# Earlier PV and projections, and residuals on VectorE, in a two-layer attention and token-mixing kernel

## The chip, the cores and the metric

The kernel runs on one core of one Trainium2 chip. The metric is the device time of that core in microseconds, from the program's start to its end. The profile's span runs from the first to the last instruction of one execution.

## The reference

The input has 2048 tokens of 1024 features in bf16. The network applies an attention block A and a token-mixing block B, and then both again with the same weights.

```
x = x + A(layernorm(x));  x = x + B(layernorm(x))      # layer 0
x = x + A(layernorm(x));  x = x + B(layernorm(x))      # layer 1

A: q, k, v = h @ wqkv      (32 heads of 32)
   a token looks at 8 tokens: itself and 2, 4, ... 14 before it
   o = softmax(q . k / sqrt(32)) v ;  result o @ wo    (1024 x 1024)
B: u = gelu(h^T @ w1 + b1)     mixes 2048 tokens into 3584
   y = u @ w2 + b2             and back into 2048 tokens
```

Since the window steps by two, even and odd tokens never meet in the attention. The kernel treats them as two classes of 1024 tokens. Block B mixes all of them.

## The kernel before

**Attention.** The class `Attn` works in four head groups per layer, numbered n = 0 to 3. Groups 0 and 1 belong to class 0, groups 2 and 3 to class 1. A group has four blocks (`dq`) of 128 features, that is four heads each. For a group the steps are:

- `qk_proj`: q and k are projected by TensorE (L400), two blocks at a time (8 units of 8 matmuls), and copied out of PSUM by ScalarE (L404, L407). There are only two q and two k buffers, so the projection of the next two blocks waits until `qk` has read these.
- `qk`: VectorE multiplies q with the shifted k (T, L430, 2.2 us, two per block), and TensorE sums over the features with a 0/1 matrix (sc, L435).
- `softmax_front` and `softmax_back`: maxima, exponentials and the quotient on VectorE and ScalarE, ending in Pb (L455). GpSimd's queue stores Pb to DRAM (pd, L458) and loads it back, spread over the partitions, in two halves (pb, L472).
- `v_proj`: v is projected (L400, four units per pair of blocks).
- `pv`: per block and half, two products of 128x2048 (L490) and then three adds that halve the width (L501, L501, L503), all on VectorE. For the pairs named in `pe_pv` the adds are eight identity matmuls (L496) and a copy by ScalarE (L498). Before the change this holds for blocks 2 and 3 of group 1 in layer 0.

`stream` writes these steps in a fixed order: during group n it does `pv` of group n-1. One exception is called `turn`: q and k of group 2, the first of class 1, are projected only after everything else of group 1. They need the normalized and transposed rows of class 1 (hT), which the fill `second` makes, so the step begins with a "drain" of `second`.

**Fills.** `weave` mixes this lead with fills, in this order once they are opened: `second` (layer 0: norm of class 1; layer 1: the last matmul of layer 0, `gemm2_tile`, for class 1), `v_ahead` (v of class 1, 16 units), `out0` (`out_proj` of class 0, eight tiles), `partials` and `late` (24 and 16 units of `gemm1` over class 0 alone). `out0` and `partials` open when `pv` of group 1 is complete. `weave` keeps two clocks, `pe` and `dve`, from costs written in each yield. Until `out0` opens, a fill is taken when TensorE's next lead unit would wait. From then on the function `even` decides:

```
pe += p
dve = max(dve, pe - AHEAD) + d
while pe < dve and pull():
    pass
```

So each unit of VectorE work is matched with TensorE fill. The costs are 1.75 of `pe` for a projection unit, 2.2 of `dve` and 0.6 of `pe` for a product T, 4.4 of `dve` for half a block of `pv` (2.3, and 1.75 of `pe`, with the adds on TensorE), 4.5 and 3.0 for the softmax. A unit of `gemm1` on one class counts 1.73, a tile of `out0` 3.9. The Tile framework then orders the instructions of each engine by this priority, and may lift a ready instruction into a gap that it foresees.

**Output projection.** `out_proj` of class 0 (`on_act`) runs eight matmuls per 128x512 half tile (L590), adds the residual by one more matmul with the identity (L593), and lets ScalarE copy the sum out with a running row sum (L594), which ScalarE's layer norm of the tile uses. `out_proj` of class 1 adds the residual on VectorE (L596). It is the end of the lead: after it come the fills that are left, and the rest of `gemm1` (L623) and `gemm2` (L649).

Of the kernel before, what the change touches and what calls it, by code (L numbers as in the profile page):

```python
# [10 lines left out]
ACT = mybir.ActivationFunctionType  # L11
ALU = mybir.AluOpType
# [14 lines left out]
def kernel(  # L27
# [13 lines left out]
    nc = tc.nc  # L41
# [4 lines left out]
    KD = D // P  # L46
# [6 lines left out]
    DQ = 4  # L53
    CH = DQ * HD
    NCQ = KD // DQ
# [8 lines left out]
    NW2 = 4  # L64
    HF = FT // NW2
    SLACK = 0.5
    AHEAD = 6.0
    assert D == H * DH and W == 8 and SC == 1024 and HD * KD == H and SB * CH == 32
    scale = float(DH) ** -0.5

# [17 lines left out]
    class at:  # L88

        def __init__(self, counter):  # L90
            self.c = counter
# [15 lines left out]
    def x2(name, shape=None, dt=BF16):  # L107
        return x2p.tile(shape or [P, D], dt, name=name, tag="x2")

    def hx(name, shape):  # L110
        return hxp.tile(shape, BF16, name=name, tag="hx")

    def wb(name, shape):
        return wbp.tile(shape, BF16, name=name, tag="wb")

    def st(name, shape):
        return stat.tile(shape, FP32, name=name, tag=name)
# [5 lines left out]
    ident = const.tile([P, P], BF16, name="ident")  # L123
# [56 lines left out]
    def rows(t):  # L180
        return t.rearrange("(i m) d -> i m d", m=P)
# [166 lines left out]

    class Attn:

        def __init__(self, li, hT, pe_pv):
            self.li, self.hT, self.pe_pv = li, hT, pe_pv
            self.oT = [[None] * KD for _ in range(DIL)]
            self.wts = {}
            self.pbs = {}
# [149 lines left out]
        def stream(self, lead):  # L505


            last = DIL * NCQ - 1
            PC = KD // 2

            def where(n, half):
                return n // NCQ, (n % NCQ) * (DQ // 2) + half

            def qk_proj(n, half):
                c, pair = where(n, half)
                if c == 1 and pair == 0:
                    yield "drain", "second"
                yield from self.proj_pair(c, pair, (1, 0))

            def v_proj(n, half):  # L520
                if n < NCQ and not (lead is not None and n == 0 and half == 0):
                    yield from self.proj_pair(*where(n, half), (2,))

            yield from lead if lead is not None else qk_proj(0, 0)
            yield "open", "second"
            yield "open", "v_ahead"
            for n in range(last + 1):
                for half in range(2):
                    nx = (n + half, 1 - half)
                    turn = nx == (NCQ, 0)  # L530
                    yield from self.qk(n, 2 * half)
                    yield from self.qk(n, 2 * half + 1)
                    if half:
                        yield from self.softmax_front()
                    if nx[0] <= last and not turn:
                        yield from qk_proj(*nx)
                    if n > 0:
                        if n - 1 == NCQ and half == 0:
                            yield "drain", "v_ahead"
                        yield from self.pv(n - 1, 2 * half)  # L540
                    if half:
                        yield from self.softmax_back(n)
                    if n > 0:
                        yield from self.pv(n - 1, 2 * half + 1)
                        if half and n - 1 == NCQ:
                            yield "open", "late"
                        if half and n - 1 == NCQ - 1:
                            yield "open", "out0"
                            yield "open", "partials"
                        if half == 0:  # L550
                            yield from v_proj(n - 1, 1)
                    if half:
                        yield from v_proj(n, 0)
                    if turn:
                        yield from qk_proj(*nx)
            yield "drain", "out0"
            for dq in range(DQ):
                yield from self.pv(last, dq)

    def out_proj(at_, c, res, dst, h2, on_act):  # L560

        dst_v = rows(dst)
        wo_t = [[None, None] for _ in range(NDC)]
        for n in range(NDC):
            for hf in range(2):
                wt = wb("wo", [P, KD // 2, 512])
                nc.sync.dma_start(out=wt[:], in_=wo_v[hf, :, :, n * 512:(n + 1) * 512])
                wo_t[n][hf] = wt
        for hf in range(2):
            h2[c][hf] = hx(f"h2{c}{hf}", [P, NT // 2, D])  # L570
        xrs = []

        def fetch():
            if len(xrs) < NT:
                xrs.append(x2("xr"))
                nc.gpsimd.dma_start(out=xrs[-1][:], in_=res[len(xrs) - 1])

        fetch()
        fetch()
        for i in range(NT):  # L580
            if not on_act:
                yield "pe", 3.5, ["oT"], [], 3.6
            xr = xrs[i]
            xn = x2("xn")
            s1 = st("s1", [P, NDC]) if on_act else None
            for n in range(NDC):
                ps = bank()
                xs_ = slice(n * 512, (n + 1) * 512)
                for kt in range(KD):
                    nc.tensor.matmul(ps[:], lhsT=at_.oT[c][kt][:, i * P:(i + 1) * P], rhs=wo_t[n][kt // 4][:, kt % 4, :],  # L590
                                     start=(kt == 0), stop=(kt == KD - 1 and not on_act))
                if on_act:
                    nc.tensor.matmul(ps[:], lhsT=ident[:], rhs=xr[:, xs_], start=False, stop=True)  # L593
                    nc.scalar.activation(out=xn[:, xs_], in_=ps[:], func=ACT.Identity, accum_out=s1[:, n:n + 1])  # L594
                else:
                    nc.vector.tensor_tensor(out=xn[:, xs_], in0=ps[:], in1=xr[:, xs_], op=ALU.add)  # L596
            fetch()
            nc.gpsimd.dma_start(out=dst_v[i], in_=xn[:])
            h = h2[c][i // 4][:, i % 4, :]
            if on_act:  # L600
                nm, rs = stats_act(xn[:], 1.0 + EPS, eps2, h, s1)
                norm_act(h, xn[:], nm, rs)
                yield 3.9, 0.0
            else:
                mean, rs = stats_dve(xn[:], 1.0 + EPS, eps2)
                norm_dve(h, xn[:], mean, rs)
# [78 lines left out]
    def weave(lead, fills):  # L685
# [20 lines left out]
        def even(p, d):  # L706
            nonlocal pe, dve
# [3 lines that stand above are left out]
# [35 lines left out]
    hT = [[None, None] for _ in range(DIL)]  # L746
    new_hT(hT, 0)
    for li in range(2):
        first = li == 0
        at_ = Attn(li, hT, {(1, 2), (1, 3)} if first else ())  # L750
        h2 = [[None, None] for _ in range(DIL)]
        res = [xin_v[c] for c in range(DIL)] if first else [rows(xb[c]) for c in range(DIL)]

# [38 lines left out]
        if first:  # L792
            with at(top):
                ln_exp_table()
            hT = [[None, None] for _ in range(DIL)]
# [38 lines left out]
```

## Time and profile before

| | us |
|---|---|
| median of 13 runs | 1336.82 |
| lowest and highest run | 1328.79, 1341.25 |
| the profiled execution | 1334.23 |
| its span | 1332.5 |
| TensorE busy | 1285.7 |
| VectorE busy | 658.1 |
| ScalarE busy | 456.7 |
| GpSimd busy | 95.2 |
| mean granted TensorE clock | 0.992 |

A timeline row gives the start, the duration, the engine, the line and operation, the count, and in brackets the idle time of the engine before it with what ended it. Durations of rows with a count run from the first start to the last end. Some matmul records are missing from the trace. Layer 0 has its attention up to about 340 us, layer 1 its own from about 590 to 990 us.

### The profile page before, as it was taken

The page shows a single profiled execution, that of the slowest core. Times are in us where ns is not written, and L with a number is a line of the kernel's source. Part 1 is how long each engine was busy: PE and PEld are TensorE (multiplying, and loading weights), DVE is VectorE, ACT ScalarE, POOL GpSimd, SP SyncE. Part 2 cuts the span into 40 slices and gives each one's busy share as a digit, 9 for nine tenths or more (in the row PEclk, how much of TensorE's full clock was granted, in tenths as well). Part 3 has the DMA queues.
Part 4 walks back from the last instruction along what each step waited for, and adds up shares of the span by engine and source line. Part 5 has one row for each costly group of instructions (what it writes and reads, how often), then busy time and mean ns, then how long its engine had stood idle before and what let it go on. Part 6 is the DMA issues. An engine that isn't in the chain of part 4 may idle for free. (4 is left out here: it accounts for less than half of the span.)

```text
span 1332.5 us, 15448 instructions
## 1 busy us (share of the span) xinstructions
PE 1285.7 (96%) x6226; PEld 582.7 (44%) x6348; DVE 658.1 (49%) x785; ACT 456.7 (34%) x808; POOL 95.2 (7%) x230
## 2 busy tenths in 40 slices
PE   8897999998999999999998999999999999999999
PEld 4343443343444444443444444444444444444444
DVE  6679597979401323325792149957971033110111
ACT  6844445931222430022624335477313144000000
POOL 3000001100100000000001100011010000000000
PEclk9998999998999999999999999999999999999999
DMA  9651525462622238873649952626444232334332
GB/s 257 139 134 63 135 83 146 154 164 72 173 64 79 77 105 212 219 183 90 180 130 220 251 152 64 159 65 180 127 128 118 63 95 71 117 91 141 117 115 61
DMA packets 239449, 173.00 MB, mean 130 GB/s; under 512 B 32209, under 2 KB 227153, under 8 KB 237329
## 3 DMA queue, kind: packets, MB, share of 16 engines
q1 hardware_dynamic: 224432, 116.67, 32.7%
q0 software_dynamic: 14368, 54.29, 14.5%
q8 instruction: 49, 0.80, 0.3%
q10 hardware_dynamic: 576, 1.05, 0.2%
q14 instruction: 24, 0.19, 0.0%
HBM read 146.81 MB, written 18.87 MB: 124 GB/s over the span
## 5 line engine op out<-in xcount | busy, mean ns | idle before, releaser
L649 PE MATMUL ps<-g,w 128*128 128x512 bf16 (+1 forms) x1781 | 388.9, 377 | 6.9 <-DMA w<-in_B_w_dram 4.8
L623 PE MATMUL ps<-h,w 128*128 128x512 bf16 x1757 | 386.4, 379 | 4.6 <-ACT h L229 2.3
L649 PEld LDWEIGHTS <-w 128*128 128x128 bf16 x1820 | 177.7, 98 | 217.5 <-issue 6.1
L623 PEld LDWEIGHTS <-w 128*128 128x128 bf16 x1792 | 175.3, 98 | 215.0 <-issue 3.6
L400 PE MATMUL ps<-hT,wq 128*128 128x512 bf16 (+1 forms) x1150 | 256.6, 376 | 3.9 <-issue 2.4
L654 DVE SCALAR_TENSOR_TENSOR xo<-ps,b_sb,xs 128x512 bf16<-128x512 f32 (+1 forms) x65 | 45.6, 738 | 297.0 <-PE ps L649 265.4
L430 DVE TENSOR_TENSOR T<-q,k 128x4096 bf16<-128x4096 bf16 x64 | 143.1, 2284 | 73.3 <-ACT q L404 53.2
L400 PEld LDWEIGHTS <-wq 128*128 128x128 bf16 x1176 | 114.4, 100 | 140.9 <-issue 17.8
L634 DVE TENSOR_TENSOR tmp<-ps,g 128x512 f32<-128x512 f32 x80 | 55.3, 691 | 210.4 <-PE ps L623 206.2
L501 DVE TENSOR_TENSOR pr<-pr 128x2048 bf16<-128x2048 bf16 x120 | 112.7, 945 | 0.5
L590 PE MATMUL ps<-wo,oT 128*128 128x512 bf16 x373 | 94.4, 383 | 8.5 <-DVE oT L503 6.1
L407 ACT CAST k<-ps 128x1024 bf16<-128x1024 f32 x64 | 64.6, 1014 | 86.9 <-PE ps L400 74.7
L490 DVE TENSOR_TENSOR pr<-pb,g 128x2048 bf16<-128x2048 bf16 x64 | 76.9, 1216 | 27.2 <-DMA pb<-pd 25.8
L400 PE MATMUL ps<-hT,wv 128*128 128x512 bf16 x376 | 87.5, 383 | 0.6 <-issue 0.2
L635 ACT ACTIVATE g<-tmp,b_sb 128x512 bf16<-128x512 f32 x80 | 57.7, 721 | 82.1 <-DVE tmp L634 82.1
L490 DVE TENSOR_TENSOR pr<-pb,v 128x2048 bf16<-128x2048 bf16 x64 | 76.1, 1213 | 8.4 <-PE ps L400 5.3
L191 ACT ACTIVATE ln<-mv,eps 128x1 f32<-128x1 f32 x37 | 10.9, 294 | 169.6 <-DVE mv L200 162.3
L629 ACT CAST g<-ps 128x512 bf16<-128x512 f32 x80 | 45.5, 588 | 66.5 <-PE ps L623 66.2
L590 PEld LDWEIGHTS <-oT 128*128 128x128 bf16 x384 | 37.5, 99 | 56.1 <-DVE oT L503 7.1
L400 PEld LDWEIGHTS <-wv 128*128 128x128 bf16 x384 | 42.7, 114 | 43.0 <-issue 6.8
L435 PE MATMUL sc<-T,sel 128*32 128x512 bf16 x512 | 39.6, 393 | 14.8 <-DVE T L430 14.5
L404 ACT CAST q<-ps 128x512 bf16<-128x512 f32 x64 | 37.0, 584 | 46.6 <-PE ps L400 46.3
(97 smaller groups left out, 642.3 us busy)
## 6 DMA issues: line engine op xcount, KB each, us to landing
w<-in_B_w_dram SPq DMA_DIRECT2D x96, 448.0 KB, 3.8
w<-in_B_w_dram SPq DMA_DIRECT2D x56, 512.0 KB, 4.8
wq<-in_A_wqkv_dram SPq DMA_DIRECT2D x40, 512.0 KB, 4.0
pb<-pd POOLq DMA_DIRECT2D x16, 1024.0 KB, 10.1
wo<-in_A_wo_dram SPq DMA_DIRECT2D x16, 512.0 KB, 3.9
xa<-xn POOLq DMA_DIRECT2D x32, 256.0 KB, 3.3
xs<-xa POOLq DMA_DIRECT2D x32, 256.0 KB, 3.5
wv<-in_A_wqkv_dram SPq DMA_DIRECT2D x12, 512.0 KB, 5.1
```

Of the source, the lines that this page charges most:

```text
L400: nc.tensor.matmul(ps[:, lo:hi], lhsT=cols, rhs=self.hT[c][hf][:, kt, lo:hi], start=(kt == 0), stop=(kt == KD - 1))
L407: nc.scalar.copy(out=window(buf, 0, PADK + hf * HT, [(KW + 1, 2), (1, HT)]), in_=ps[:].unsqueeze(1).to_broadcast([P, 2, HT]))
L430: nc.vector.tensor_tensor(out=T[:], in0=q[:].unsqueeze(1).to_broadcast([P, 4, SC]), in1=window(k, par, 2, [(2, 4), (1, SC)]), op=ALU.mult)
L490: nc.vector.tensor_tensor(out=pr[:, :, u, :], in0=pb[:, :, u, :], in1=window(v, par, 2 + hf * HT, [(TB, 4), (2, 4), (1, TB)]), op=ALU.mult)
L501: nc.vector.tensor_tensor(out=pr[:, :, 0:wd, :], in0=pr[:, :, 0:wd, :], in1=pr[:, :, wd:2 * wd, :], op=ALU.add)
L590: nc.tensor.matmul(ps[:], lhsT=at_.oT[c][kt][:, i * P:(i + 1) * P], rhs=wo_t[n][kt // 4][:, kt % 4, :], start=(kt == 0), stop=(kt == KD - ...
L623: nc.tensor.matmul(ps[:], lhsT=wt[c][:, i, fl * P:(fl + 1) * P], rhs=h2[c][i // 4][:, i % 4, dc * 512:(dc + 1) * 512], start=(k == 0), sto ...
L629: nc.scalar.copy(out=gs, in_=ps[:])
L634: nc.vector.tensor_tensor(out=tmp[:], in0=ps[:], in1=gs, op=ALU.add)
L635: nc.scalar.activation(out=gs, in_=tmp[:], func=ACT.Gelu_apprx_tanh, bias=b1_sb[:, ft:ft + 1])
L649: nc.tensor.matmul(ps[:, 0:xc.stop - xc.start], lhsT=w2t[n][:, ft % HF, c::DIL], rhs=g[ft // GF][:, ft % GF, xc], start=(ft == 0), stop=(f ...
L654: nc.vector.scalar_tensor_tensor(out=xo[:, xc], in0=ps[:, 0:xc.stop - xc.start], scalar=b2_sb[:, i, c:c + 1], in1=xs[:, xc], op0=ALU.add, ...
```

## The change

- In layer 1 the whole `pv` of group 1 (and the v projection of its last two blocks) is written ahead of class 1's first q and k projection, and `out0` and `partials` open there (`ahead`, `early = DQ`).
- In layer 0 the q and k projection of group 2 takes its regular place behind `softmax_front` of group 1 (`turn` is false there), and no `pv` has its adds on TensorE.
- In `out_proj` of class 0, of both layers, the identity matmul goes, and VectorE adds the residual in one instruction that also gives the row sum.
- The planner's AHEAD goes from 6 to 10, and a tile of `out0` counts 3.5.

```diff
-    AHEAD = 6.0
+    AHEAD = 10.0
...
-        def __init__(self, li, hT, pe_pv):
-            self.li, self.hT, self.pe_pv = li, hT, pe_pv
+        def __init__(self, li, hT, pe_pv, early):
+            self.li, self.hT, self.pe_pv, self.early = li, hT, pe_pv, early
...
+            def opened_by(n):
+                if n == NCQ - 1:
+                    yield "open", "out0"
+                    yield "open", "partials"
+                elif n == NCQ:
+                    yield "open", "late"
+
+            def ahead():
+                c, pair = where(NCQ - 1, 1)
+                for dq in range(self.early):
+                    if dq == DQ // 2:
+                        for dt in (2 * pair, 2 * pair + 1):
+                            for hf in range(2):
+                                yield from self.proj(c, 2, dt, hf)
+                    yield from self.pv(NCQ - 1, dq)
+                if self.early == DQ:
+                    yield from opened_by(NCQ - 1)
+
...
             for n in range(last + 1):
+                done = self.early if n == NCQ else 0
                 for half in range(2):
                     nx = (n + half, 1 - half)
-                    turn = nx == (NCQ, 0)
+                    turn = nx == (NCQ, 0) and self.li > 0
                     yield from self.qk(n, 2 * half)
                     yield from self.qk(n, 2 * half + 1)
                     if half:
                         yield from self.softmax_front()
                     if nx[0] <= last and not turn:
                         yield from qk_proj(*nx)
-                    if n > 0:
-                        if n - 1 == NCQ and half == 0:
-                            yield "drain", "v_ahead"
+                    if n - 1 == NCQ and half == 0:
+                        yield "drain", "v_ahead"
+                    if n > 0 and 2 * half >= done:
                         yield from self.pv(n - 1, 2 * half)
                     if half:
                         yield from self.softmax_back(n)
-                    if n > 0:
+                    if n > 0 and 2 * half + 1 >= done:
                         yield from self.pv(n - 1, 2 * half + 1)
-                        if half and n - 1 == NCQ:
-                            yield "open", "late"
-                        if half and n - 1 == NCQ - 1:
-                            yield "open", "out0"
-                            yield "open", "partials"
-                        if half == 0:
-                            yield from v_proj(n - 1, 1)
+                        if half:
+                            yield from opened_by(n - 1)
+                    if n > 0 and half == 0 and done <= DQ // 2:
+                        yield from v_proj(n - 1, 1)
                     if half:
                         yield from v_proj(n, 0)
+                    if nx == (NCQ, 0):
+                        yield from ahead()
                     if turn:
                         yield from qk_proj(*nx)
...
-                                     start=(kt == 0), stop=(kt == KD - 1 and not on_act))
+                                     start=(kt == 0), stop=(kt == KD - 1))
                 if on_act:
-                    nc.tensor.matmul(ps[:], lhsT=ident[:], rhs=xr[:, xs_], start=False, stop=True)
-                    nc.scalar.activation(out=xn[:, xs_], in_=ps[:], func=ACT.Identity, accum_out=s1[:, n:n + 1])
+                    nc.vector.scalar_tensor_tensor(out=xn[:, xs_], in0=ps[:], scalar=1.0, in1=xr[:, xs_], op0=ALU.mult,
+                                                   op1=ALU.add, accum_out=s1[:, n:n + 1])
...
-                yield 3.9, 0.0
+                yield 3.5, 0.0
...
-        at_ = Attn(li, hT, {(1, 2), (1, 3)} if first else ())
+        at_ = Attn(li, hT, (), 0 if first else DQ)
```

## Prediction

> **What bounds the kernel now.** I read the page first.
>
> ```profile
> span 1332.5 us, 15448 instructions
> ...
> PE 1285.7 (96%) x6226; PEld 582.7 (44%) x6348; DVE 658.1 (49%) x785; ACT 456.7 (34%) x808; POOL 95.2 (7%) x230
> ...
> PE   8897999998999999999998999999999999999999
> ...
> DVE  6679597979401323325792149957971033110111
> ```
>
> TensorE is busy for 96%, and its dents lie where VectorE's digits are high: the attention stages. Outside them only TensorE's own work counts, and the change leaves that alone. Its pace is read from `out0` in TensorE's timeline: half tiles of 9 matmuls start at 226.48, 228.42 and 230.37 us, so one matmul costs 1.945 / 9 = 0.216 us.
>
> Next, who ends TensorE's waits, and where VectorE waits in layer 0 (rows of the waits, then of VectorE's timeline):
>
> ```profile
> PE sc L435 <- DVE T L430: 14.5, 13, 4.2
> PE ps L590 <- DVE oT L503: 6.1, 2, 3.7
> PE ps L649 <- DMA w<-in_B_w_dram: 4.8, 2, 3.0
> PE ps L623 <- ACT h L229: 2.3, 2, 1.9
> ```
>
> ```profile
> 156.21 8.90 DVE L430 TENSOR_TENSOR T<-q,k 128x4096 bf16<-128x4096 bf16 x4 [13.95 <-ACT q L404]
> ...
> 219.61 2.36 DVE L490 TENSOR_TENSOR pr<-pb,g 128x2048 bf16<-128x2048 bf16 x2 [3.38 <-DMA pb<-pd]
> 225.61 1.23 DVE L490 TENSOR_TENSOR pr<-pb,g 128x2048 bf16<-128x2048 bf16 x1 [3.64 <-DMA pb<-pd]
> ...
> 282.73 2.36 DVE L490 TENSOR_TENSOR pr<-pb,g 128x2048 bf16<-128x2048 bf16 x2 [8.77 <-DMA pb<-pd]
> ```
>
> The first of these is the cost of `turn`: VectorE stands still while TensorE runs what is left of `v_ahead` and only then q and k of group 2. The others are the way of Pb through DRAM. Behind the last, VectorE works without a break until 318.9 us, and TensorE waits for it:
>
> ```profile
> 316.68 0.61 PE L590 MATMUL ps<-wo,oT 128*128 128x512 bf16 x1 [3.75 <-DVE oT L503]
> ...
> 708.00:775.00 67.00, 61.88 (x274) 27.57 (x279) 8.99 (x14) 24.87 (x57) 7.87 (x20) 0.97 0.99 249
> ```
>
> So in layer 0 the end of attention is VectorE's, and ten units of `gemm1` (236 of 320 matmul records stand ahead of it) are left for later. In layer 1 TensorE is nearly full throughout, and the second row, of the windows, shows 67 us in which VectorE has 9 us of work: the drain of `second`.
>
> **The change part by part.** Prices (groups, shapes apart):
>
> ```profile
> L501 DVE TENSOR_TENSOR pr<-pr 128x2048 bf16<-128x2048 bf16 x60 | 72.7, 1211 | 0.3
> L654 DVE SCALAR_TENSOR_TENSOR xo<-ps,b_sb,xs 128x512 bf16<-128x512 f32 x63 | 44.6, 746 | 292.2 <-PE ps L649 260.5 <-DMA xs<-xa 20.9 <-issue 10.7
> L594 ACT ACTIVATE xn<-ps 128x512 bf16<-128x512 f32 x32 | 18.7, 584 | 12.5 <-PE ps L593 11.5 <-issue 1.0
> L594 ACT ACTIVATION_READ_ACCUMULATOR xn<-ps 128x1 f32 x32 | 6.1, 192 | 0.0
> ```
>
> *TensorE loses* 32 matmuls L496 in layer 0 and 16 matmuls L593 in each layer: 64 x 0.216 = 13.8 us, of it 10.4 in layer 0. That is worth time only if TensorE doesn't wait instead.
>
> *PV adds back on VectorE, layer 0.* Four halves of blocks, each with adds that start 1.14, 0.60 and 0.34 us apart in VectorE's timeline: 4 x 2.08 = 8.3 us more. ScalarE loses four copies of 0.58, which cover nothing.
>
> *Residuals on VectorE.* 16 per layer. The nearest row is L654, the same operation on the same shapes, 0.746 us, but without a row sum. The Trainium skill (VectorE: DVE Perf Modes, section "Two Vector instructions with no wait between them") says that an operation which also writes out its accumulator is two instructions, the main one and an accumulator read. ScalarE's rows show such a read at 0.192 us; no row shows VectorE's. By the row alone the 16 cost 11.9 us per layer, by the rule 16 x 0.94 = 15.0. I take 15.0. ScalarE is relieved of 2 x (0.584 + 0.192) = 1.55 us per tile, so tiles of h2 come sooner if VectorE isn't late. PSUM banks are now freed by VectorE: behind a PV that waits for pb, three tiles would fill the six banks. GpSimd's store of xa now waits for VectorE too, with Pb's store and the pb loads queued behind it. Both come from VectorE's one stream, so I price the queue at 0, and up to 3 us if a residual is late.
>
> *q and k of group 2 earlier, layer 0.* Its 64 matmuls (13.8 us) and two 512 KB loads on SP's queue go ahead of PV's second half and `v_proj`. hT is there: `v_ahead`, which reads it, already runs. The products T can then start at about 142.2 instead of 156.2: 13.95 us off VectorE's chain. What is late next: pb of group 1, whose loads are issued at 143.3 and land in 7 to 13 us, so its second half may hold VectorE between 0 and 6 us; I take 2. Later, since VectorE's adds take the place of TensorE's, Pb of group 2 isn't the last thing finished, and the 7.0 us wait at 216 to 226 shrinks by 5 (2 to 7).
>
> VectorE's chain to the end of layer 0's attention: -14 + 2 + 8.3 - 5 + 15 - 2 (residuals that fall into what is left of the waits; 0 to 8) = +4.3 us, between -5 and +12.
>
> *Fill, layer 0.* At the opening of `out0` the planner's `dve` minus `pe` was 4.5 + 4 x 2.3 + 3 - (14 + 7) = -4.3; it becomes 4.5 + 4 x 4.4 + 3 - 14 = +11.1. From there to the last PV `dve` gains 95.5 (8 T, 16 PV, softmax), `pe` 18.8, and the jump of 14 past AHEAD adds 8 before and 4 after. Fill ahead of class 1's `out_proj`: 80.4 before, 91.8 after. Less `out0` (31.2, 28.0), that is 28 units of `gemm1` (the trace has 30) against 37. Of the 9 more, `v_ahead` may take up to 6, since fewer of its units are needed around the old `turn`. I take 5 units of 1.73: 8.6 us of TensorE's later work moves under VectorE's chain. Layer 0: +4.3 - 8.6 = -4.3 us. That is how 10.4 us of saved matmuls come to less than half.
>
> *Layer 1.* 16 halves of PV (8 x 4.4 = 35 us) move from the crowded 798 to 878 us into the empty 708 to 775. They need pb of group 1 (about 722 us); 35 us and the four remaining pairs of L654 end before `second` does. SP's queue gets two v loads of 512 KB among the w2 loads in a stretch whose DMA share is 0.99, where TensorE already lost 1.85 and 2.95 us; up to 4 us, and I take 0, since 6.9 us of projections come along to cover them. Gains: 16 x 0.216 = 3.5; the waits for oT (2.3) and h (1.9) at the end. Against it: `even` now starts a whole group earlier, and after a projection of 14 it gives no fill until `dve` has made up AHEAD. So none stands between q and k of groups 2 and 3, where each projection waits for T (two per buffer, 4.5 us) three times: 0 to 13 us, by how much Tile lifts `v_ahead` in. I take 3.7. Layer 1: -3.5 - 4.2 + 3.7 = -4.0 us, between -11 and +6.
>
> Sum: -8.3 us. The profiled execution took 1334.2 (span 1332.5 and 1.7 around it), so 1326 for such a one; it lies 2.6 below the median of the runs shown, and against that I say 1328.5.
>
> **The rivals.** *All of it arrives* (0.20): Tile fills the gaps that it foresees, so 13.8 us of matmuls and some 8 us of waits vanish: 1315. For it: fine-grained mixing of fills in TensorE's timeline. Against: VectorE, not TensorE, ends layer 0's attention.
>
> *VectorE's chain outgrows its cover* (0.22, slower): in layer 0 between 142 and 319 us, residuals at 0.94 us and pb's second half landing late make the chain 12 us longer, while `v_ahead` takes most of the added fill (3 units, 5 us): +7 there, with layer 1 at zero: 1344. It decides once the chain grows by more than 8.6 + 4 = 12.6 us against 5 units, or 9 against 3. For it: VectorE is busy for 167 of 201 us there already. Against: the 14 us wait is real and structural.
>
> *Nothing moves* (0.13): the removed waits return as TensorE waits for T without fill in layer 1 (13 instead of 3.7): 1338. That the change doesn't do what it says would show as L593 or L496 left; I see no way to it.
>
> **How the numbers follow.** The likeliest case has 0.45 and 1321 to 1334 as its own range. Within 0.3% (4 us, about what a measurement of this kernel tells from no change) lies 0.05 of it. Faster: 0.40 + 0.20 = 0.60; same 0.05 + 0.13 = 0.18; slower 0.22. The range takes in both rivals: 1314 to 1344.
>
> **What would show it.** No L496 and L593; the 13.95 us wait ahead of T near 156 us gone, one on pb in its place; residual rows near 0.75 with a read behind; 33 to 37 units of `gemm1` ahead of class 1's `out_proj` in layer 0, whose wait for oT stays; VectorE busy with L490 at 722 to 765 us. I am wrong if layer 0's attention ends over 10 us later than 319, or if TensorE's waits for T exceed 25 us (14.5 before).

## The result and the profile after

| | before | after |
|---|---|---|
| median, us | 1336.27 (48 runs) | 1325.35 (11 runs, 1321.17 to 1330.35) |
| ratio to before, 95% interval | | 0.992 (0.9905 to 0.9936) |
| the profiled execution, its span | 1334.2, 1332.5 | 1327.2, 1325.4 |

The forecast was 1328.5. The page's rows of busy time and of the slices:

```profile
PE 1276.3 (96%) x6163; PEld 576.8 (44%) x6284; DVE 687.3 (52%) x861; ACT 438.4 (33%) x740; POOL 95.4 (7%) x230
...
PE   8997998999999999999998999999799999999999
...
DVE  6669898979502422244796646667970033111111
```

TensorE's records hold 9.4 us less work, VectorE's 29 us more. In slices 22 to 24, where layer 1's early PV now lies, VectorE's digits are 664 (214 before), in the three behind them 666 (995 before), and TensorE has one new dent, a 7, in slice 29. The waits show what the dent is (line, what it waited for, us in total, times, longest):

```profile
PE sc L435 <- DVE T L430: 14.1, 12, 4.5
PE ps L608 <- DVE oT L503: 10.7, 3, 7.0
...
PE ps L667 <- DMA w<-in_B_w_dram: 0.6, 1, 0.6
```

The waits for w2 fell from 4.8 to 0.6 us, those for T stayed (14.5 before), and the waits for oT rose from 6.1 to 10.7. L608 is now the matmul of `out_proj`, L641 `gemm1`, L667 `gemm2`, L611 the new residual.

**Two stretches.** The first score product of layer 1 (first row of `sc` in TensorE's timeline after 560 us) divides the span. Its row in before, then in after:

```profile
599.89 0.61 PE L435 MATMUL sc<-T,sel 128*32 128x512 bf16 x8
```

```profile
591.25 0.61 PE L435 MATMUL sc<-T,sel 128*32 128x512 bf16 x8
```

Layer 0 gained 8.6 us. From that row to the end of the span it is 732.6 us before and 734.2 after: layer 1 took 1.5 us more. The table of the experiments has this stretch between 732.6 and 735.4 us where layer 1 is as in after or nearly so; so a loss isn't certain, but nothing was gained there. All of the gain is layer 0's.

**Layer 0.** VectorE's timeline of after, at the old 13.95 us wait, at a residual, and around the old wait for pb:

```profile
140.07 2.27 DVE L430 TENSOR_TENSOR T<-q,k 128x4096 bf16<-128x4096 bf16 x1
...
202.25 0.67 DVE L611 SCALAR_TENSOR_TENSOR xn<-ps,xr 128x512 bf16<-128x512 f32 x1
202.85 0.07 DVE L611 DVE_READ_ACCUMULATOR xn<-ps,xr 128x1 f32 x1
202.85 1.21 DVE L501 TENSOR_TENSOR pr<-pr 128x2048 bf16<-128x2048 bf16 x1
...
217.03 0.69 DVE L611 SCALAR_TENSOR_TENSOR xn<-ps,xr 128x512 bf16<-128x512 f32 x1 [3.59 <-DMA xa<-xn]
```

T of group 2 starts at 140.07, not 156.21, and the wait is gone; 3.40 us came back at 150.39, where T waits for `sc` to have read its buffer. A residual and its accumulator read take 0.60 us from start to start (202.25 to 202.85). The 7.0 us of waits for pb at 216 to 226 became one of 3.59, not for pb: the residual needs the xn buffer that GpSimd's store of xa is still reading.

The end of the attention, in TensorE's timeline of after, and the weight loads of `gemm1` that stand ahead of it (one load for each matmul, 8 to a unit, so they count units without the trace's gaps; before, then after, each for layer 0 and layer 1):

```profile
318.97 0.39 PE L608 MATMUL ps<-wo,oT 128*128 128x512 bf16 x1 [2.99 <-DVE oT L503]
```

```profile
L623 PEld LDWEIGHTS <-w x240: 95/98/98, 258.5 to 310.8; 128*128 128x128 bf16 x120
L623 PEld LDWEIGHTS <-w x240: 95/98/98, 909.6 to 963.6; 128*128 128x128 bf16 x120
```

```profile
L641 PEld LDWEIGHTS <-w x296: 95/98/99, 247.6 to 313.9; 128*128 128x128 bf16 x148
L641 PEld LDWEIGHTS <-w x232: 95/98/98, 897.2 to 948.3; 128*128 128x128 bf16 x116
```

The reader sees 30 and 30 units before, 37 and 29 after. In layer 0 VectorE's chain ends 2.3 us later (318.97 against 316.68 at this row), and seven more units, 7 x 1.73 = 12.1 us, lie under it: 2.3 - 12.1 = -9.8, near the measured -8.6. Counted as TensorE's work instead, 48 matmuls of 0.216 us have left layer 0, 10.4 us; the two counts describe the same gain.

**Layer 1.** The same place, in TensorE's timeline of before and then of after, and the granted clock there in after (a row of the windows; the column after POOL is the clock):

```profile
964.86 0.81 PE L590 MATMUL ps<-wo,oT 128*128 128x512 bf16 x3
968.01 0.39 PE L590 MATMUL ps<-wo,oT 128*128 128x512 bf16 x1 [2.34 <-DVE oT L503]
```

```profile
949.56 0.81 PE L608 MATMUL ps<-wo,oT 128*128 128x512 bf16 x3
957.37 0.61 PE L608 MATMUL ps<-wo,oT 128*128 128x512 bf16 x1 [7.00 <-DVE oT L503]
957.77 1.91 PE L608 MATMUL ps<-wo,v 128*128 128x512 bf16 x4
...
961.18 1.07 PE L608 MATMUL ps<-wo,v 128*128 128x512 bf16 x4
```

```profile
957.00:962.00 5.00, 4.63 (x13) 1.77 (x14) 4.43 (x7) 0.00 (x0) 0.00 (x0) 0.57 0.00 0
```

Counted from the layer's first score product, TensorE reaches this row's neighbours 6.7 us sooner than before (949.56 - 591.25 = 358.3 against 365.0), but the last oT is there only 2.0 us sooner (366.1 against 368.1). So the wait grew by 4.7. The nine matmuls from the end of the wait to 961.18 took 3.8 us where before they took 1.95, at a granted clock of 0.57. And one unit of `gemm1` more was left for later, 1.73 us. Sum: -2.0 + 1.86 + 1.73 = +1.6, measured +1.5 in these two profiles. TensorE did lose its work; it was spent on waiting for VectorE.

Why VectorE's chain gained only 2 us though 35 us of PV had left it is in its own timeline, of before and then of after:

```profile
789.39 8.89 DVE L430 TENSOR_TENSOR T<-q,k 128x4096 bf16<-128x4096 bf16 x4 [10.33 <-ACT q L404]
...
933.44 2.36 DVE L490 TENSOR_TENSOR pr<-pb,g 128x2048 bf16<-128x2048 bf16 x2 [7.55 <-DMA pb<-pd]
...
938.59 1.22 DVE L490 TENSOR_TENSOR pr<-pb,g 128x2048 bf16<-128x2048 bf16 x1 [1.53 <-DMA pb<-pd]
```

```profile
787.27 8.89 DVE L430 TENSOR_TENSOR T<-q,k 128x4096 bf16<-128x4096 bf16 x4 [10.27 <-ACT q L404]
...
844.77 2.36 DVE L490 TENSOR_TENSOR pr<-pb,g 128x2048 bf16<-128x2048 bf16 x2 [9.06 <-ACT g L407]
...
921.93 2.36 DVE L490 TENSOR_TENSOR pr<-pb,g 128x2048 bf16<-128x2048 bf16 x2 [6.64 <-DMA pb<-pd]
927.95 1.23 DVE L490 TENSOR_TENSOR pr<-pb,g 128x2048 bf16<-128x2048 bf16 x1 [2.40 <-DMA pb<-pd]
```

The first T of group 2 comes 196.0 us after the layer's start, where it came after 189.5 before: 6.5 us later, about the four units of v (6.9 us) that now go ahead of class 1's q and k. From there to the last oT VectorE's waits add up to 43.6 us, 27.6 before. New are those for TensorE: for q of the next two blocks (7.69), for v of class 1 (9.06), for `out0`'s matmuls ahead of residuals (2.27 at 867.89, the first of several); one of 12.77 us for `sc` is gone. The wait for pb ahead of the last PV is not new: 9.08 us before, 9.04 after. Which of these costs time was open, and is what most experiments ask.

### The profile page after: what moved, and what is told of

Its sections match the earlier page's. It is cut to its first block, busy times and chain, and to the rows that moved or that the text cites. A ratio compares the mean times of both kernels' runs of the same rounds, so it can differ in the third digit from the quotient of the medians.

```text
span 1325.4 us, 15310 instructions
## 1 busy us (share of the span) xinstructions
PE 1276.3 (96%) x6163; PEld 576.8 (44%) x6284; DVE 687.3 (52%) x861; ACT 438.4 (33%) x740; POOL 95.4 (7%) x230
## 5 line engine op out<-in xcount | busy, mean ns | idle before, releaser
L641 PE MATMUL ps<-h,w 128*128 128x512 bf16 x1754 | 387.5, 379 | 5.6 <-ACT h L229 1.4
L667 PE MATMUL ps<-g,w 128*128 128x512 bf16 (+1 forms) x1781 | 387.2, 376 | 2.7 <-DMA w<-in_B_w_dram 0.6
L400 PE MATMUL ps<-hT,wq 128*128 128x512 bf16 (+1 forms) x1149 | 262.9, 381 | 7.2 <-ACT v L407 2.0
L641 PEld LDWEIGHTS <-w 128*128 128x128 bf16 x1792 | 175.0, 98 | 217.3 <-issue 6.2
L667 PEld LDWEIGHTS <-w 128*128 128x128 bf16 x1820 | 177.5, 98 | 211.4 <-issue 3.8
L501 DVE TENSOR_TENSOR pr<-pr 128x2048 bf16<-128x2048 bf16 (+1 forms) x128 | 119.9, 944 | 0.3
L608 PE MATMUL ps<-wo,oT 128*128 128x512 bf16 x374 | 91.1, 385 | 12.3 <-DVE oT L503 10.7
L608 PEld LDWEIGHTS <-oT 128*128 128x128 bf16 x384 | 37.5, 99 | 60.6 <-DVE oT L503 12.2
L435 PE MATMUL sc<-T,sel 128*32 128x512 bf16 x512 | 39.9, 394 | 14.1 <-DVE T L430 14.1
```

The source lines that it names most:

```text
L400: nc.tensor.matmul(ps[:, lo:hi], lhsT=cols, rhs=self.hT[c][hf][:, kt, lo:hi], start=(kt == 0), stop=(kt == KD - 1))
L501: nc.vector.tensor_tensor(out=pr[:, :, 0:wd, :], in0=pr[:, :, 0:wd, :], in1=pr[:, :, wd:2 * wd, :], op=ALU.add)
L641: nc.tensor.matmul(ps[:], lhsT=wt[c][:, i, fl * P:(fl + 1) * P], rhs=h2[c][i // 4][:, i % 4, dc * 512:(dc + 1) * 512], start=(k == 0), sto ...
L667: nc.tensor.matmul(ps[:, 0:xc.stop - xc.start], lhsT=w2t[n][:, ft % HF, c::DIL], rhs=g[ft // GF][:, ft % GF, xc], start=(ft == 0), stop=(f ...
```

## The experiments

Every ratio is to the kernel before, run on the same chip. The profiles of each kernel divide at the same row as above:

| kernel | median (runs) | ratio, 95% interval | start of layer 1 | from there to the end | units ahead, layer 0 / 1 | wait for the last oT, layer 0 / 1 |
|---|---|---|---|---|---|---|
| before | | 1 | 599.9 | 732.6 | 30 / 30 | 3.75 / 2.34 |
| after | 1325.35 (11) | 0.992 (0.9905 to 0.9936) | 591.3 | 734.2 | 37 / 29 | 2.99 / 7.00 |
| after_again | 1325.72 (6) | 0.9936 (0.9914 to 0.9958) | 588.6 | 734.6 | 37 / 29 | 2.41 / 7.13 |
| e1, residuals alone | 1331.99 (14) | 0.9983 (0.9969 to 0.9997) | 601.6 | 732.4 | 32 / 32 | 4.53 / 1.84 |
| e2, no early PV | 1327.92 (6) | 0.9958 (0.9942 to 0.9974) | 590.3 | 737.5 | 37 / 29 | 3.13 / 6.33 |
| e3, turn back | 1337.88 (16) | 1.0026 (1.0014 to 1.0037) | 602.0 | 734.2 | 40 / 29 | 1.35 / 6.92 |
| e4, AHEAD 6 | 1325.11 (7) | 0.9933 (0.9908 to 0.9958) | 595.7 | 728.6 | 40 / 32 | 1.52 / 2.42 |
| e5, four v first | 1326.67 (6) | 0.9945 (0.9931 to 0.996) | 588.9 | 734.1 | 37 / 29 | 2.66 / 5.64 |
| e6, PV adds on TensorE | 1330.93 (22) | 0.9979 (0.9968 to 0.9989) | 595.6 | 732.6 | 29 / 29 | 5.84 / 5.69 |
| e7, residuals on TensorE | 1330.23 (10) | 0.9973 (0.9959 to 0.9988) | 590.7 | 734.0 | 35 / 28 | 1.73 / 2.27 |
| e8, v split | 1326.89 (8) | 0.9939 (0.9914 to 0.9964) | 588.1 | 734.6 | 37 / 21 | 2.70 / 8.18 |
| e9, four units taken | 1326.16 (6) | 0.9942 (0.9922 to 0.9962) | 588.0 | 735.4 | 37 / 29 | 3.12 / 7.32 |
| e10, NPART 11 | 1323.44 (6) | 0.9916 (0.9898 to 0.9934) | 588.6 | 733.6 | 37 / 29 | 2.64 / 7.06 |
| e11, 8 us lag | 1315.88 (4) | 0.9853 (0.983 to 0.9876) | 587.5 | 726.4 | 37 / 34 | 3.01 / none |

The start of layer 1 lies between 587.5 and 591.3 in the profiles of the seven kernels whose layer 0 is after's (after, after_again, e2, e5, e8, e9, e11), so 4 us of that column is scatter; against the one profile of before, layer 0's gain is 8.6 to 12.4 us. The column beside it scatters by some 3 us: 732.6 to 735.4 for after, after_again, e3, e5, e6, e8, e9 and e10, whose layer 1 is after's or differs little in its plan.

### The parts undone one by one

**e2: no early PV in layer 1.**

```diff
-        at_ = Attn(li, hT, (), 0 if first else DQ)
+        at_ = Attn(li, hT, (), 0)
```

> The changed kernel with the PV of group 1 in layer 1 back in its old place; all else changed. Theory A (layer 1's VectorE chain, which now carries 16 residuals, was kept short by moving 35 us of PV into the empty stretch): the chain's end in layer 1 comes 8 to 12 us later than the 957 us of the changed kernel, some of it covered by fill, so 1330 to 1336. Theory B (layer 1 took 734 us from its first sc to the end where it took 733 before, so moving PV there was worth nothing): 1325, within 3.

1327.92 us, 0.9958: about 5 us slower than after at 0.992, but 3 us against after's second measurement, so its size is loose. The profile shows it where it should lie: layer 1 is 3.3 us longer than after's (737.5), 2.1 more than the longest of the others. Its waits:

```profile
PE ps L608 <- DVE oT L503: 10.2, 3, 6.3
PE ps L667 <- DMA w<-in_B_w_dram: 4.9, 2, 2.8
```

The waits for w2 are back at 4.9. The forecast had them covered by the projections that come along with the early PV; e2 takes both away, so the two aren't told apart. The long wait for oT is there without the early PV, so the early PV isn't its cause.

**e3: turn back in layer 0.**

```diff
-                    turn = nx == (NCQ, 0) and self.li > 0
+                    turn = nx == (NCQ, 0)
```

> The changed kernel with q and k of group 2 in layer 0 projected last again, as before the change. Theory A (VectorE's chain sets the end of layer 0's attention): the wait of some 14 us ahead of T is back, the 3.4 us wait that stands there now goes, the chain's end moves from 321 to about 331 us: 1332 to 1336. Theory B (TensorE's work sets the pace, the wait only moves): 1325 to 1328.

1337.88 us, 1.0026: 12 to 14 us slower by the ratios of after's two measurements, and 10.8 in the profiles, all in layer 0 (602.0). That is theory A, somewhat above its range. VectorE's timeline of it, and then TensorE's:

```profile
156.22 2.29 DVE L430 TENSOR_TENSOR T<-q,k 128x4096 bf16<-128x4096 bf16 x1 [13.95 <-ACT q L404]
```

```profile
363.12 0.59 PE L641 MATMUL ps<-h,w 128*128 128x512 bf16 x1 [4.68 <-DVE h L224]
```

The wait returns to the hundredth, the chain ends 10.2 us later (329.13 at the row of the last oT), and one thing was not expected: with all 40 units used up under the longer chain, nothing is left to cover the norm of the last tile behind `out_proj`, and TensorE waits 7.4 us for h.

**e6: the adds of two blocks of PV back on TensorE in layer 0.**

```diff
-        at_ = Attn(li, hT, (), 0 if first else DQ)
+        at_ = Attn(li, hT, {(1, 2), (1, 3)} if first else (), 0 if first else DQ)
```

> The changed kernel with the adds of blocks 2 and 3 of group 1 in layer 0 on TensorE again. Theory A (TensorE's saved matmuls are time, as with the residuals, and the planner's two clocks open nearer together, so fewer units of gemm1 lie under VectorE's chain): 6.9 us of matmuls come back, 4 to 8 us slower than the changed kernel. Theory B (VectorE's chain in layer 0 decides, and it gets 8.3 us shorter): 3 us faster or more.

1330.93 us, 0.9979: 5.7 us slower than after on the same chip (0.9936). Its last oT is there at 312.11 us, after a wait of 5.84. The weight loads ahead of it:

```profile
L641 PEld LDWEIGHTS <-w x232: 95/98/98, 252.8 to 304.2; 128*128 128x128 bf16 x116
```

VectorE's chain is 6.9 us shorter, and the kernel is slower: the planner, told of less VectorE work, puts only 29 units ahead instead of 37, and TensorE waits 5.84 us. A shorter chain was worth nothing here, where the fill that was to lie under it went. The 32 identity matmuls that come back are 6.9 us of TensorE work by themselves, about the whole loss; e6 changes both and doesn't separate them.

**e7: residuals of class 0 back on TensorE and ScalarE.** `out_proj` as before (L593, L594, 3.9), all else as after.

```diff
-                                     start=(kt == 0), stop=(kt == KD - 1))
+                                     start=(kt == 0), stop=(kt == KD - 1 and not on_act))
...
+                    nc.tensor.matmul(ps[:], lhsT=ident[:], rhs=xr[:, xs_], start=False, stop=True)
+                    nc.scalar.activation(out=xn[:, xs_], in_=ps[:], func=ACT.Identity, accum_out=s1[:, n:n + 1])
-                    nc.vector.scalar_tensor_tensor(out=xn[:, xs_], in0=ps[:], scalar=1.0, in1=xr[:, xs_], op0=ALU.mult,
-                                                   op1=ALU.add, accum_out=s1[:, n:n + 1])
...
-                yield 3.5, 0.0
+                yield 3.9, 0.0
```

> The changed kernel with class 0's residuals again as an identity matmul on TensorE and a copy by ScalarE; all else changed. Theory A (VectorE's chains end both attentions): TensorE gets 6.9 us more, VectorE's chains get 11 us shorter in each layer, the waits for oT (3.0 and 7.0 us) go: 1319 to 1326. Theory B (saved matmuls are time): 1331 to 1333.

1330.23 us, 0.9973: 5 to 7 us slower by the ratios of after's two measurements, near the 6.9 us of 32 matmuls of 0.216, as theory B has it. Both waits for oT shrink, to 1.73 and 2.27, but TensorE has a new one, for xr, which GpSimd's queue brings late:

```profile
215.70 0.58 PE L611 MATMUL ps<-xr,ident 128*128 128x512 bf16 x1 [4.41 <-DMA xr<-in_A_x_dram]
```

The profiled execution, 1326.6 us, was among the quickest of this kernel's runs (1325.84 to 1332.49), and its stretches show none of the loss (590.7 and 734.0), so where it lies isn't shown; the ratio rests on the medians.

**e1: the residuals alone, on the kernel before.** The change of `out_proj` and the 3.5, nothing else.

```diff
-                                     start=(kt == 0), stop=(kt == KD - 1 and not on_act))
+                                     start=(kt == 0), stop=(kt == KD - 1))
...
-                    nc.tensor.matmul(ps[:], lhsT=ident[:], rhs=xr[:, xs_], start=False, stop=True)
-                    nc.scalar.activation(out=xn[:, xs_], in_=ps[:], func=ACT.Identity, accum_out=s1[:, n:n + 1])
+                    nc.vector.scalar_tensor_tensor(out=xn[:, xs_], in0=ps[:], scalar=1.0, in1=xr[:, xs_], op0=ALU.mult,
+                                                   op1=ALU.add, accum_out=s1[:, n:n + 1])
...
-                yield 3.9, 0.0
+                yield 3.5, 0.0
```

> The kernel before with only the residuals of class 0 on VectorE (and a tile of out0 counted at 3.5). Theory A (saved matmuls are time only where TensorE doesn't wait for VectorE's chain, which gets 11 us longer per layer, some of it in VectorE's waits, and in layer 0 fills are not moved under it): from 3 us faster to 4 slower, ratio 0.998 to 1.003. Theory B (as undoing it from the changed kernel says: 7 us): 5 to 8 us faster, ratio 0.994 to 0.996.

1331.99 us, 0.9983: 2.3 us won (0.4 to 4.1), less than half of what undoing the same part costs on top of the others. Its profiled execution is the slowest of its 14 (1335.74), so its stretches are long. With VectorE's chain still carrying the 14 us wait, its waits are `sc` for T 17.0 (14.5 before) and 4.53 for oT (3.75 before). So the parts are not additive: undone singly they cost 3 to 5, 12 to 14, 6 to 8 and 5 to 7 us, by the one or the other measurement of after, 26 to 34 together, while all four brought 11. The likely reading is that each is worth its matmuls or its wait only where the others keep TensorE supplied.

**e4: AHEAD back to 6.**

```diff
-    AHEAD = 10.0
+    AHEAD = 6.0
```

> The changed kernel with AHEAD at 6 again; all else changed. Theory A (fills are only put in other places, and TensorE is full there in any case): within 3 us of the changed kernel; in layer 0 two units more of gemm1 stand ahead of class 1's output projection, 39 for 37. Theory B (a lower AHEAD puts v of class 1 ahead of group 3's projections in layer 1 and VectorE's waits there go): 6 to 9 us faster. Theory C (10 was needed, since with 6 fills crowd in before VectorE's chain): 4 us slower or more.

1325.11 us, 0.9933, against 0.9936 for after on that chip: the same. But the stretches say that this is two effects that cancel: layer 0 is 7.1 us longer (595.7 against 588.6), layer 1 is 6.0 us shorter (728.6 against 734.6). Its weight loads of layer 0 and layer 1:

```profile
L641 PEld LDWEIGHTS <-w x320: 95/98/100, 246.9 to 319.4; 128*128 128x128 bf16 x160
L641 PEld LDWEIGHTS <-w x256: 95/98/98, 900.9 to 957.3; 128*128 128x128 bf16 x128
```

A smaller AHEAD gives three more units before `out_proj` in each layer. Layer 1 had a long wait to put them in (7.1 to 2.4). Layer 0 had a short one (2.4), ran out of units and waits 7.5 us for h (1.0 in after). So layer 1 lacks fill at its end, and AHEAD at 10 is what took it. The layer 1 of e1 and that of e2 say the same, since they differ in AHEAD alone, 6 in e1 and 10 in e2:

```profile
L623 PEld LDWEIGHTS <-w x256: 95/98/98, 912.7 to 969.0; 128*128 128x128 bf16 x128
L641 PEld LDWEIGHTS <-w x232: 95/98/98, 899.9 to 951.7; 128*128 128x128 bf16 x116
```

That is 32 units against 29, a wait for oT of 1.84 against 6.33 and 732.4 against 737.5 us. In `even` a larger AHEAD lets `dve` start further behind `pe`, so less fill is called for. AHEAD 6 in layer 1 with 10 in layer 0 was not run; the stretches of e4 and after_again would make a span of 588.6 + 728.6 = 1317 us, an estimate.

**after_again** is the kernel after beside e4, e6 and e8.

> The changed kernel itself, as the mark for the runs beside it: ratio to the kernel before 0.992, inside 0.9905 to 0.9936, and again a wait for oT of some 7 us in layer 1 and 3 us in layer 0. A ratio above 0.995 would say that differences of a quarter of a per cent between kernels can't be read here.

0.9936 (0.9914 to 0.9958), with the wait for oT at 7.13 us: layer 1 ends in the same wait each time.

### What layer 1 lacks

**e5: four units of v taken early**, so that the 9.06 us wait for v goes.

```diff
+                    if n == NCQ + 1 and half == 0 and self.li > 0:
+                        yield "take", 4
                     if nx[0] <= last and not turn:
                         yield from qk_proj(*nx)
...
+            elif kind == "take":
+                for _ in range(unit[0]):
+                    pull()
```

> The changed kernel, and in layer 1 four units of v of class 1 are taken ahead of the q and k projection of the last group's second pair. Theory A (in layer 1 VectorE lost 9.06 us at 844.77 waiting for v of class 1, since no fill was planned ahead of it, and this became TensorE's 7.0 us wait for oT and the slow matmuls after it): both waits go, 1316 to 1319. Theory B (6.9 us more in front of q and k push T back by as much): 1325 to 1330.

1326.67 us, 0.9945: nothing gained. VectorE's timeline shows where it went:

```profile
866.61 0.69 DVE L613 SCALAR_TENSOR_TENSOR xn<-ps,xr 128x512 bf16<-128x512 f32 x1 [8.73 <-PE ps L610]
```

The wait for v is gone, and the residual of `out0` (L613 in this kernel) stands at the head of VectorE's queue for 8.73 us instead, until TensorE gets to `out0`. VectorE waits for TensorE's sequence here in any case.

**e8: v of class 1 split**, its last two pairs behind `out0`.

```diff
+                    if self.li > 0:
+                        yield "open", "v_rest"
...
             yield "drain", "out0"
+            yield "drain", "v_rest"
...
-        def v_ahead():
-            for t in v_g:
+        def v_ahead(lo, hi):
+            for t in v_g[2 * lo:2 * hi]:
...
-            for pair in range(KD // 2):
+            for pair in range(lo, hi):
...
-        weave(lead, {"second": second_class(), "v_ahead": v_ahead(),
+        weave(lead, {"second": second_class(), "v_ahead": v_ahead(0, 4 if first else 2), "v_rest": v_ahead(2, 4),
```

> The changed kernel; in layer 1 v of class 1 is split: the first 8 units before PV of group 2 as now, then out0, and the other 8 units behind it, before PV of group 3. Theory A (VectorE stands in layer 1 first for v and then, when v comes earlier, for the first residual of out0, which sits in its queue ahead of T: 26 us of v in one piece on TensorE keep both back): out0 starts some 14 us sooner, VectorE's waits fall by 8 to 10 us, the wait for oT of 7 us goes: 6 to 9 us faster than the changed kernel. Theory B (the chain is held by something later, such as pb of group 3): within 3 us of it.

1326.89 us, 0.9939: the same as after. This one separates the two readings. VectorE's chain ended some 13 us sooner (940.79 less the layer's start is 352.7, against 366.1), and yet TensorE's wait for it grew to 8.18 us. The weight loads:

```profile
L644 PEld LDWEIGHTS <-w x168: 97/98/98, 894.5 to 930.5; 128*128 128x128 bf16 x168
```

Only 21 units stood ahead instead of 29; the other eight, 13.8 us, came later, since the eight units of v now lie under the chain in their place (880 to 895 us). The length of VectorE's chain doesn't set layer 1's time by itself: the wait that it leaves does, and that depends on how much fill is planned under it.

**e9: four units of `gemm1` taken ahead of the last PV in layer 1** (the `take` of e5, at another place).

```diff
             yield "drain", "out0"
+            yield "take", 4 if self.li > 0 else 0
```

> The changed kernel, and in layer 1 four units of gemm1 more (6.9 us of TensorE) are taken just before PV of group 3. Theory A (the wait for oT is what the plan leaves uncovered: `even` counts VectorE's work but not its 7 to 9 us wait for pb, so TensorE arrives early by as much, whatever the chain's length; 11 units are left for later anyway): the 7.0 us wait and the slow matmuls behind it go, 7 to 9 us faster than the changed kernel, 1316 to 1319 against 1336 before, ratio 0.985 to 0.988. Theory B (units taken there need weight buffers that the output projection's weights want, so a wait for loads comes instead): within 3 us of the changed kernel.

1326.16 us, 0.9942, 29 units ahead and a wait of 7.32 us: no change, and no answer. A unit pulled by `take` advances the clock `pe`, so `even` gave as many fewer afterwards. The dose wasn't given, and the theory not tested.

**e10: NPART 11**, a constant of the fills, with `take` of 4 and 3 units at the same place.

```diff
-    NPART = 10
+    NPART = 11
...
             yield "drain", "out0"
+            yield "take", 4 if self.li > 0 else 3
```

> As the kernel with four units more in layer 1, and also 11 instead of 10 column blocks of gemm1 that are begun over class 0 alone, in both layers, and three units taken before PV of group 3 in layer 0. Theory A: the 3.0 us wait for oT in layer 0 goes too and enough units stay behind it to cover the last tile's norm: 2 to 5 us faster than the kernel without this, ratio 0.981 to 0.986. Theory B (the eleventh block's place in SBUF is v of class 1's fifth block, which PV of group 3 still reads, so its units stand in TensorE's queue waiting for VectorE): equal to it or slower, by up to 9 us.

1323.44 us, 0.9916 (0.9898 to 0.9934): within after's interval. The units ahead are 37 and 29 as in after, the wait in layer 1 is 7.06. Again no dose by `take`.

**e11: the planner is told of the wait for pb.** 8 us are added to its VectorE clock ahead of the last group's PV in layer 1.

```diff
             yield "drain", "out0"
+            yield "lag", 8.0 if self.li > 0 else 0.0
...
+            elif kind == "lag":
+                if unit[0]:
+                    dve = max(dve, pe - AHEAD) + unit[0]
```

> The kernel after, with 8 us added to the planner's VectorE account ahead of the last group's PV in layer 1 (the wait for pb, which the account doesn't know), so that five more units of gemm1 (5 x 1.73 = 8.6 us; 34 instead of 29) stand ahead of class 1's out_proj. Here the dose is given for certain, unlike with the four units taken directly. Theory A (layer 1's loss is a wait of 7.0 us for the last oT, and some 2 us of slow matmuls behind it, that the plan leaves uncovered): the wait at about 957 us falls below 1 us, the slow matmuls behind it go, and the kernel is 6 to 9 us faster than the kernel after: 1316 to 1320 us, a ratio to the kernel before of 0.985 to 0.988. Theory B (VectorE's stream or the weights limit the stretch all the same: the moved units wait for h or for PSUM banks, or push VectorE's chain behind them): the oT wait stays over 3 us or comes back at other lines, and the ratio is 0.990 to 0.995, within 3 us of the kernel after.

1315.88 us (1315.36 to 1317.17), 0.9853 (0.983 to 0.9876): 9.5 us faster than after's median, and apart from its interval. Weight loads, then TensorE's timeline and the windows at the old wait (L609 and L642 are after's L608 and L641):

```profile
L642 PEld LDWEIGHTS <-w x272: 95/98/98, 894.7 to 954.4; 128*128 128x128 bf16 x136
```

```profile
944.69 10.31 PE L642 MATMUL ps<-h,w 128*128 128x512 bf16 x47
954.83 1.03 PE L609 MATMUL ps<-wo,v 128*128 128x512 bf16 x4
```

```profile
940.00:957.00 17.00, 17.00 (x81) 7.69 (x80) 16.19 (x21) 5.35 (x10) 0.00 (x0) 1.00 0.24 79
```

34 units ahead, no wait, no slow matmuls, TensorE busy for 17.00 of 17 us at full clock (10.32 at 0.92 in after). Layer 1 takes 726.4 us, 7.8 less than after and outside the scatter of that stretch; the rest of the 9.5 lies in the scatter of layer 0's. The kernel was expected to gain 6 to 9. VectorE's 9 us wait for v stays (9.12 in its timeline), so it costs nothing by itself. What e11 shows is that fill was missing: the lag was sized by the wait for pb, but that wait was there in before too, with only 2.34 us of wait for oT.

This version is the fastest of all: 1.5% below before, 0.7% below after.

## Why the prediction was right, and where it was not

The time, 1328.5 against 1325.35, and the direction hold. Its two halves do not: -4.3 and -4.0 us were forecast, and -8.6 (or up to -12.4) and about +1.5 came. That their sum came within 3.2 us of the forecast is luck: two errors of opposite sign.

**Right in layer 0.** The 13.95 us wait is gone as forecast, and e3 returns it to the hundredth: the lever was the place of q and k of group 2. VectorE's chain ends 2.3 us later; +4.3 was forecast. The wait for oT stays (2.99). The form of the gain, units of `gemm1` moved under a chain that hardly changes, fits the counts (37 units, 30 before) and e6, where a shorter chain over 29 units is slower; e6 brings 6.9 us of matmuls back as well and so doesn't prove it.

**Mis-sized in layer 0: the units.** The planner's arithmetic gave nine more units, of which I took five, leaving four to `v_ahead`. Seven came, 12.1 us instead of 8.6. That term (3.5 us) and the chain's (2.0) make up the difference to -4.3, and 1.2 more than came.

**Mis-sized: the residual.** I took 0.94 us by the rule that an accumulator read is an instruction of its own (the Trainium skill, VectorE: DVE Perf Modes, "Two Vector instructions with no wait between them") and by ScalarE's 0.192 for such a read. The rule's form is right: DVE_READ_ACCUMULATOR has its row. But it takes 0.07 to 0.08 us and starts with the next operation, and a pair takes 0.60 to 0.61 us from start to start. 16 of them are 9.7 us per layer, not 15.0; the row without the rule (11.9) was nearer. The saving of 5.3 was partly offset: the wait at 216 to 226 shrank by 3.4 and not by 5, and `sc` took 3.4 where pb was to take 2.

**Wrongly priced at 0 there: GpSimd's store of xa.** The new wait of 3.59 us at 217 is for the xn buffer that this store reads. The bound of 3 us that stood beside the 0 was nearer.

**Failed: layer 1, step by step.**

- The 16 matmuls left (3.5 us), and the early PV lies where forecast: VectorE is busy for 42.96 us of the stretch from 708 to 775 (8.99 before).
- "The waits for oT (2.3) and h (1.9) at the end" were to vanish. This is the step that failed. The wait for oT rose to 7.00, with 1.9 us of slow matmuls behind it. I took a shorter VectorE chain for granted because 35 us of PV left it, and counted no fill in layer 1 as I had in layer 0. The chain is 2.0 us shorter, since it starts 6.5 us later and waits 16 us longer on its way; and e8 shows that a chain 13 us shorter still didn't help. What counts is the fill planned up to its end. The smaller count of an `out0` tile should have raised it (32 units in e1, 30 before), but AHEAD at 10 takes three units away (29 in e2 and in after). With AHEAD back at 6, e4's layer 1 takes 728.6 us: 4.0 less than before, by one profile of each, and the gain that was forecast. So the part of the change that cost layer 1 its gain is AHEAD. It makes the long wait only together with the residuals on VectorE: e7, without these, waits 2.27 us, but its layer 1 is no shorter (734.0), with 16 matmuls more and 28 units.
- The forecast did have a term for AHEAD, 3.7 us, but as waits for T between q and k of groups 2 and 3. They did not come: 14.1 us of waits for T in all against 14.5. The lost fill was missed at the end of the chain instead.
- e11 makes up for it in another way: 8 us in the planner's account give five units, and 7.8 us come back. The plan has no entry for the 9 us wait for pb ahead of the last PV, but it had none in before either, so that is not what the change made worse.
- The w2 loads, priced at 0 and up to 4, gained: the waits fell from 4.8 to 0.6 (2.0 in after_again), and e2 brings them back. 3.5 us of new waits for wq (1.5) and v (2.0) stand against that.

**The rivals.** *All of it arrives* missed the bound in layer 1. In layer 0 it was near: 8.6 to 12.4 us came, and 10.4 us of matmuls had left, though VectorE still ends the attention there. *VectorE's chain outgrows its cover* was wrong on the place, since layer 0's chain grew by 2.3 and not by 12. In layer 1 the wait for the chain did grow, by 4.7, from too little fill. *Nothing moves* is refuted by the waits for T.

Still open: how the 2 to 3 us that divide e10 from after would come out with more runs, what AHEAD set for each layer would give, and what e11's lag would give in layer 0, where 3.01 us of wait are left; these were not tried.

## What to carry to other kernels

When two engines are matched by a plan written in costs, count the fill that stands under the end of each chain, before and after, for every stage: work removed elsewhere turns into waiting where the fill is short. A constant of the plan that helps one stage (AHEAD in layer 0) can take as much from another, and a line in the account (e11) can be worth almost as much as the change itself. Divide the span at a common event before judging a result near the forecast: two errors of opposite sign, as here and in e4, look like a success or like no effect. Undo parts one at a time as well as doing one alone: the four here cost 26 to 34 us undone and brought 11 together.

## What the runs showed of the hardware that was not expected

- VectorE's accumulator read took 0.07 to 0.08 us and ran beside what follows (both rows start at 202.85); ScalarE's took 0.192 in before. A row sum on VectorE was nearly free here.
- A short wait of TensorE can cost more than itself. After 7.00 us, eight matmuls started 0.43 us apart instead of 0.216 (1.9 us in sum). The waits for oT in these profiles fall into two: after those of 2.41 us and more matmuls were slow, for some 3 to 5 us, and after those of 1.35 to 2.34 us none were. But length alone doesn't decide it, as TensorE's row of the windows shows for after, behind its wait of 1.99 us for v at 721.99:

```profile
722.00:725.00 3.00, 3.00 (x8) 1.12 (x8) 3.00 (x5) 0.98 (x1) 0.00 (x0) 0.55 0.96 160
```

The granted clock is 0.55 there. The Trainium skill (TensorE: Matmul & The Clock Gate, "What's actually happening") has the clock halved after at least one idle window of about 3.4 us, at no fixed phase to the kernel; here waits of 1.99 to 2.99 us were followed by it too. The 2.99 us in layer 0 of after cost 4.7 us in all: the 17 matmuls up to 324.33 us took 1.7 us more than 17 of 0.216.
